# A gated convolution on one core: three weight loads and one output weight, all issued by ScalarE ahead of its table load

## The chip, the cores and the metric

One core of a Trainium2 chip. The metric is device time in microseconds of one execution, median of several runs of the same kernel. A profile is one further execution, recorded by the hardware profiler. It has a span (first to last instruction of the program) that is a little shorter than the device time.

TensorE multiplies, VectorE and ScalarE do elementwise work and move results out of the accumulator banks, GpSimd does a share of the elementwise work, and SyncE only issues transfers. ScalarE can issue transfers too. SyncE's transfers run on the queue that the profile calls q1, ScalarE's on q10.

## The reference

A causal convolution over time with three taps and a dilation of 2, a gate, and an output projection. With B = 2, T = 16000, D = 256, all in bf16:

```python
xp = jnp.pad(x, ((0, 0), (4, 0), (0, 0)))
h  = einsum(xp[:, 4:4+T], w[0]) + einsum(xp[:, 2:2+T], w[1]) + einsum(xp[:, 0:T], w[2])
f, g = h[..., :D], h[..., D:]
z  = tanh(f) * sigmoid(g)
out = z @ w_o
```

`w[k]` is 256 x 512 (256 KB), `w_o` is 256 x 256 (128 KB).

## The kernel before

A row is four time steps, with the phases 0 to 3. Phases 0 and 1 are called x, phases 2 and 3 y; with a dilation of 2, each output of x needs x of its row, y of the row before (`yp`) and x of the row before (`xp`), and each output of y needs y and x of its row and `yp`. Rows are handled in groups of 256 (128 at some ends), and one group of 256 rows is one 512-column product. Channels lie on the partitions, which needs x transposed. That is done by transposing transfers: `load_chunk` (L96 to L108) issues one on SyncE's queue at L105 for each chunk of one or two groups. The first group's 128 rows are handled in another way: they are loaded plainly into `xn` (L117), transposed by TensorE (`turn`, L136 to L143) and copied by ScalarE and VectorE into the first chunk's tile.

The three taps of two outputs are computed with four products and not six. For each group VectorE and GpSimd form the difference m (`pre_m`, L155), the sum p (`pre_p`, L161) and further differences d (`pre_d`, L172). The weights of these products are made once from the taps: `wd0` = 2 w0 and `wd2` = 2 w2 on ScalarE (L363, L364), `wt` = w0 + w2, `wm` = wt - w1 and `wp` = wt + w1 on VectorE (L365 to L367). `products` (L197) multiplies m into a bank b and p into a bank a; `copy_m2` (ScalarE, L227) copies b; `combine` (VectorE, L234 and L235) writes a - copy into b and a + copy into a; then `products` adds d with `wd0` into b and d with `wd2` into a. So TensorE's second pair of products for a block waits for VectorE's combine. A block is 128 of the 512 output channels of a group, four blocks to a group. `activate` (ScalarE, L248) applies tanh or sigmoid, `gate` (VectorE, L266) multiplies, `out_mm` (TensorE, L287) projects with `wo_sb`, and `out_evict` (L306, L308) copies the result out and issues its transfer on SyncE.

The first group (four blocks) doesn't use m, p and d. `direct` (L216) multiplies its rows by the three taps as they come: tap 2 first, then tap 0, then tap 1 (`TAPS = (2, 0, 1)`, L47).

The order of instructions on each engine is the order in which the code is written (`manual_schedule`). The head of the kernel, by engine:

- SyncE issues xn, then tap 0 (L121), then the transposing transfers of chunks 1 and 2 (L105). A third one waits in the loop for its buffer.
- ScalarE issues tap 2 and tap 1 (L119), loads its activation table (L120), copies two of the four turned pieces of x (L143), scales two taps (L363, L364), activates block 0, issues w_o (L375) and activates on.
- VectorE copies the other two pieces of x (L143), makes wt, wm and wp (L365 to L367), then m and p of group 1 (L155, L161), three of its differences, and the first combine.
- TensorE runs 28 products on zeros (L92), turns x (L141), multiplies blocks 0 to 2 by the taps and block 3 by the first two, then takes the m and p products of block 4, the rest of block 3, and in the loop those of blocks 5 and 6 ahead of the d products of block 4.

Each transfer has its own semaphore, and the first instruction on each engine that reads what it loads waits for it.

Of the kernel before, what the change touches and what calls it, by code (L numbers as in the profile page):

```python
# [13 lines left out]
def kernel(  # L14
# [19 lines left out]
    nc = tc.nc  # L34
# [4 lines left out]
    P = 128  # L39
# [7 lines left out]
    TAPS = (2, 0, 1)  # L47
# [41 lines left out]
    def warm_up(n):  # L89
        wps = ps_a.tile([P, 2 * RG], f32, name="a")  # L90
        for _ in range(n):
            nc.tensor.matmul(wps[:, :P], lhsT=warm[:], rhs=warm[:], start=True, stop=True)  # L92
# [20 lines left out]
    w_taps = [consts.tile([P, CT, D2], bf16, name=f"w{k}_sb") for k in range(K)]  # L113
    wo_sb = consts.tile([P, NT, D], bf16)
    xn = consts.tile([P, 4, D], bf16, name="xn")
    w_in = [w[k].rearrange("(ct c) d -> c ct d", c=P) for k in range(K)]
    nc.sync.dma_start(out=xn[:], in_=x[0, 0:4 * P, :].rearrange("(r j) c -> r j c", j=4))  # L117
    for k in (TAPS[0], TAPS[2]):
        nc.scalar.dma_start(out=w_taps[k][:], in_=w_in[k])  # L119
    nc.scalar.preload_act_table(ACT.Sigmoid)  # L120
    nc.sync.dma_start(out=w_taps[TAPS[1]][:], in_=w_in[TAPS[1]])  # L121
    warm_up(N_WARM[0])
    ident = consts.tile([P, P], bf16)
    make_identity(nc, ident[:])
# [56 lines left out]
    def products(k, which):  # L181
        g, oi = divmod(k, 4)
        G = groups[g]
        o = O_ORDER[oi]
        osl = slice(o * P, (o + 1) * P)
        R = G["R"]
        N = 2 * R
        if which in (1, 2):
            G["ab"[which - 1], oi] = (ps_a, ps_b)[which - 1].tile([P, 2 * RG], f32, name="ab"[which - 1])
        wmat, mv, bank, first = {  # L190
            2: (wm_sb, lambda ct: G["m"][:, :, ct, :R], "b", True),
            1: (wp_sb, lambda ct: G["p"][:, :, ct, :R], "a", True),
            3: (wd0_sb, lambda ct: G["d"][:, 2:4, ct, :R], "b", False),
            0: (wd2_sb, lambda ct: G["d"][:, 0:2, ct, :R], "a", False),
        }[which]
        for ct in range(CT):
            nc.tensor.matmul(  # L197
                G[bank, oi][:, :N], lhsT=wmat[:, ct, osl], rhs=mv(ct),
                start=first and ct == 0, stop=ct == CT - 1, skip_group_check=True,
            )  # L200
# [21 lines left out]
    def copy_m2(k):  # L222
        g, oi = divmod(k, 4)
        G = groups[g]
        N = 2 * G["R"]
        G["ss", oi] = ss_pool.tile([P, 2 * RG], f32, name="ss")
        nc.scalar.copy(out=G["ss", oi][:, :N], in_=G["b", oi][:, :N])  # L227
# [9 lines left out]
    def activate(k):  # L237
        g, oi = divmod(k, 4)
        G = groups[g]
        R = G["R"]  # L240
        o = O_ORDER[oi]
        if oi == 0:
            G["th"] = act_pool.tile([P, NT, 4, RG], bf16, name="th")
            G["sg"] = act_pool.tile([P, NT, 4, RG], bf16, name="sg")
            G["z"] = z_pool.tile([P, NT, 4, RG], bf16, name="zz")
        dst = G["th"][:, o] if o < NT else G["sg"][:, o - NT]
        for h, bank in ((1, "b"), (0, "a")):
            nc.scalar.activation(  # L248
                out=dst[:, 2 * h:2 * h + 2, :R],
                in_=G[bank, oi][:, :2 * R].rearrange("p (q r) -> p q r", q=2),  # L250
                func=ACT.Tanh if o < NT else ACT.Sigmoid, scale=1.0 if g == 0 else 0.5,
            )
# [118 lines left out]
    direct(3, TAPS[:-1])  # L371
    products(N_DIRECT, 2)
    products(N_DIRECT, 1)
    activate(0)
    nc.scalar.dma_start(out=wo_sb[:], in_=w_o.rearrange("(ct c) d -> c ct d", c=P))  # L375
    activate(1)
    activate(2)
    copy_m2(N_DIRECT)
    for part in range(3):
        last = pre_d(1, part, nc.vector)  # L380
# [8 lines left out]
    k = N_DIRECT + 1  # L389
# [81 lines left out]
```

## Time and profile before

| | us |
|---|---|
| median of 3 runs | 284.5 (284.37 to 284.89) |
| the profiled execution | 284.21 |
| its span | 282.4 |
| ScalarE busy | 261.0 |
| VectorE busy | 243.2 |
| GpSimd busy | 126.2 |
| TensorE's granted clock | 0.999 of full speed |

A trace lists each instruction with its engine, source line, start and length, the idle time before it and what ended that. For transfers it gives the issue on the issuing engine, the time from the start of the issue to the landing (when the semaphore is complete), and the traffic of each queue in any stretch of time. A matmul's end is modelled, so successive matmuls overlap in the listing; the distance between their starts is what one costs. "Issue" as a releaser means that the engine waited for nothing that the profile shows.

### The profile page before, as it was taken

The page shows a single profiled execution, that of the slowest core. Times are in us where ns is not written, and L with a number is a line of the kernel's source. Part 1 is how long each engine was busy: PE and PEld are TensorE (multiplying, and loading weights), DVE is VectorE, ACT ScalarE, POOL GpSimd, SP SyncE. Part 2 cuts the span into 40 slices and gives each one's busy share as a digit, 9 for nine tenths or more (in the row PEclk, how much of TensorE's full clock was granted, in tenths as well). Part 3 has the DMA queues.
Part 4 walks back from the last instruction along what each step waited for, and adds up shares of the span by engine and source line. Part 5 has one row for each costly group of instructions (what it writes and reads, how often), then busy time and mean ns, then how long its engine had stood idle before and what let it go on. Part 6 is the DMA issues. An engine that isn't in the chain of part 4 may idle for free.

```text
span 282.4 us, 4903 instructions
## 1 busy us (share of the span) xinstructions
PE 277.7 (98%) x1641; PEld 160.3 (57%) x1641; DVE 243.2 (86%) x417; ACT 261.0 (92%) x533; POOL 126.2 (45%) x136
## 2 busy tenths in 40 slices
PE   8999999999999999999999999999999999999994
PEld 8644555555555555556854555555555555555782
DVE  3999888888888888888999988888888888888884
ACT  5598999999999999999999999999999999999994
POOL 1145454455445444533564544554455445443430
PEclk9999999999999999999999999999999999999999
DMA  7887291723718145092793614709345152321223
GB/s 219 191 182 153 75 194 74 172 95 93 184 64 172 67 104 90 37 223 77 183 266 76 171 42 118 182 37 183 121 104 163 50 151 77 79 75 74 77 88 110
DMA packets 76440, 34.55 MB, mean 122 GB/s; under 512 B 66944, under 2 KB 68480, under 8 KB 76416
## 3 DMA queue, kind: packets, MB, share of 16 engines
q1 hardware_dynamic: 75600, 33.59, 48.1%
q10 hardware_dynamic: 816, 0.66, 0.7%
q8 instruction: 13, 0.21, 0.3%
q14 instruction: 11, 0.09, 0.1%
HBM read 1.18 MB, written 16.38 MB: 62 GB/s over the span
## 4 chain that ended last, share of the span: by engine, by line
PE 98%; DVE 0%; DVEq 0%; issue 0%
PE a L197 38%; PE b L197 38%; PE o_ps L287 19%; PE a L92 1%; PE a L216 1%; PE b L216 1%; PE tp L141 0%; PE a L332 0%; DVE osb_end L339 0%; PE b L332 0%; DVEq L466 0%; DVE warm L112 0%
## 5 line engine op out<-in xcount | busy, mean ns | idle before, releaser
L172 POOL TENSOR_TENSOR dd<-xt 128x512 bf16<-128x512 bf16 (+2 forms) x128 | 125.4, 980 | 146.2 <-DVE zz L266 65.5
L234 DVE TENSOR_TENSOR b<-a,ss 128x512 f32<-128x512 f32 (+2 forms) x132 | 87.4, 662 | 30.4 <-ACT ss L227 27.4
L235 DVE TENSOR_TENSOR a<-a,ss 128x512 f32<-128x512 f32 (+2 forms) x132 | 86.2, 653 | 0.0
L227 ACT COPY ss<-b 128x512 f32<-128x512 f32 (+2 forms) x132 | 73.9, 560 | 11.6 <-ACT th L248 0.9
L197 PEld LDWEIGHTS <-wd_sb 128*128 128x128 bf16 x528 | 51.5, 98 | 55.2 <-issue 0.8
L197 PE MATMUL a<-dd,wd_sb 128*128 128x512 bf16 (+2 forms) x264 | 74.7, 364 | 0.0
L197 PE MATMUL b<-dd,wd_sb 128*128 128x512 bf16 (+2 forms) x264 | 74.7, 364 | 0.0
L197 PE MATMUL a<-pp,wp_sb 128*128 128x512 bf16 (+2 forms) x264 | 74.7, 364 | 0.0
L197 PE MATMUL b<-mm,wm_sb 128*128 128x512 bf16 (+2 forms) x264 | 74.7, 364 | 0.0
L287 PE MATMUL o_ps<-wo_sb,zz 128*128 128x256 bf16 x488 | 73.2, 273 | 0.0
L306 ACT CAST osb<-o_ps 128x512 bf16<-128x512 f32 x121 | 72.0, 595 | 0.0
L287 PEld LDWEIGHTS <-zz 128*128 128x128 bf16 x488 | 47.7, 98 | 28.1
L266 DVE TENSOR_TENSOR zz<-th,sg 128x1024 bf16<-128x1024 bf16 (+1 forms) x67 | 43.1, 644 | 0.0
L248 ACT ACTIVATE th<-b 128x512 bf16<-128x512 f32 (+2 forms) x68 | 39.7, 584 | 2.7 <-PE b L197 1.6
L197 PEld LDWEIGHTS <-wp_sb 128*128 128x128 bf16 x264 | 25.8, 98 | 27.3 <-DVE pp L161 0.2
L248 ACT ACTIVATE sg<-b 128x512 bf16<-128x512 f32 (+2 forms) x68 | 39.6, 583 | 0.5 <-PE b L216 0.3
L248 ACT ACTIVATE th<-a 128x512 bf16<-128x512 f32 (+2 forms) x68 | 39.8, 585 | 0.0
L248 ACT ACTIVATE sg<-a 128x512 bf16<-128x512 f32 (+2 forms) x68 | 39.7, 583 | 0.0
L197 PEld LDWEIGHTS <-wm_sb 128*128 128x128 bf16 x264 | 25.8, 98 | 4.5
L161 DVE TENSOR_TENSOR pp<-xt 128x1024 bf16<-128x1024 bf16 (+2 forms) x33 | 21.8, 662 | 0.0
L155 DVE TENSOR_TENSOR mm<-xt 128x1024 bf16<-128x1024 bf16 (+2 forms) x33 | 21.5, 650 | 0.3 <-DMA xt<-in_x_dram 0.3
L216 PEld LDWEIGHTS <-w_sb 128*128 128x128 bf16 x48 | 4.6, 98 | 1.0 <-issue 0.2
(35 smaller groups left out, 36.7 us busy)
## 6 DMA issues: line engine op xcount, KB each, us to landing
out_dram<-osb SPq DMA_DIRECT2D x61, 256.0 KB, 2.1
w_sb<-in_w_dram ACTq DMA_DIRECT2D x2, 256.0 KB, 4.3
xt<-in_x_dram SPq DMA_TRANSPOSE x18, 6.7
xn<-in_x_dram SPq DMA_DIRECT2D x1, 256.0 KB, 3.0
w_sb<-in_w_dram SPq DMA_DIRECT2D x1, 256.0 KB, 4.1
out_dram<-osb_end SPq DMA_DIRECT2D x2, 128.0 KB, 1.9
wo_sb<-in_w_o_dram ACTq DMA_DIRECT2D x1, 128.0 KB, 4.9
out_dram<-osb_odd SPq DMA_DIRECT2D x8, 16.0 KB, 3.0
```

The source lines that it names most:

```text
L155: return nc.vector.tensor_tensor(out=G["m"][:, :, :, :G["R"]], in0=xc, in1=yp, op=ALU.subtract)
L161: return nc.vector.tensor_tensor(out=G["p"][:, :, :, :G["R"]], in0=xc, in1=yp, op=ALU.add)
L172: ins = eng.tensor_tensor(out=G["d"][:, j, :, :R], in0=a[:, q], in1=s[:, q], op=ALU.subtract)
L197: nc.tensor.matmul(G[bank, oi][:, :N], lhsT=wmat[:, ct, osl], rhs=mv(ct), start=first and ct == 0, stop=ct == CT - 1, skip_group_check=True,)
L216: nc.tensor.matmul(G[bank, oi][:, :2 * R], lhsT=w_taps[tap][:, ct, osl], rhs=mv[:, :, ct, :], start=tap == TAPS[0] and ct == 0, stop=tap = ...
L227: nc.scalar.copy(out=G["ss", oi][:, :N], in_=G["b", oi][:, :N])
L234: nc.vector.tensor_tensor(out=pb[:, :N], in0=pa[:, :N], in1=ss[:, :N], op=ALU.subtract)
L235: nc.vector.tensor_tensor(out=pa[:, :N], in0=pa[:, :N], in1=ss[:, :N], op=ALU.add)
L248: nc.scalar.activation(out=dst[:, 2 * h:2 * h + 2, :R], in_=G[bank, oi][:, :2 * R].rearrange("p (q r) -> p q r", q=2), func=ACT.Tanh if o ...
L266: return nc.vector.tensor_tensor(out=G["z"][:, dt, :, :full], in0=G["th"][:, dt, :, :full], in1=G["sg"][:, dt, :, :full], op=ALU.mult)
L287: nc.tensor.matmul(o_ps[:, q, :], lhsT=lhsT, rhs=wo_sb[:, dt, :], start=(dt == 0), stop=(dt == NT - 1),)
L306: copy(out=osb[:, 2 * jp:2 * jp + 2, :], in_=o_ps[:])
```

## The change

Two edits. At the start, the load of tap 0 leaves SyncE's queue and is issued by ScalarE between tap 2 and tap 1 (its three issues then stand in the order 2, 0, 1), and the load of w_o is issued by ScalarE right behind them, ahead of the load of the activation table. SyncE's queue then holds xn and behind it the transposing transfers. Later, the w_o load between the activations of blocks 0 and 1 is gone.

```diff
     nc.sync.dma_start(out=xn[:], in_=x[0, 0:4 * P, :].rearrange("(r j) c -> r j c", j=4))
-    for k in (TAPS[0], TAPS[2]):
+    for k in TAPS:
         nc.scalar.dma_start(out=w_taps[k][:], in_=w_in[k])
+    nc.scalar.dma_start(out=wo_sb[:], in_=w_o.rearrange("(ct c) d -> c ct d", c=P))
     nc.scalar.preload_act_table(ACT.Sigmoid)
-    nc.sync.dma_start(out=w_taps[TAPS[1]][:], in_=w_in[TAPS[1]])
     warm_up(N_WARM[0])
...
-    activate(0)
-    nc.scalar.dma_start(out=wo_sb[:], in_=w_o.rearrange("(ct c) d -> c ct d", c=P))
-    activate(1)
-    activate(2)
+    for k in range(3):
+        activate(k)
     copy_m2(N_DIRECT)
```

The order of all instructions that compute stays the same on every engine.

## The prediction

> **What bounds the kernel now.** I read the page first: busy times and the chain that ended last.
>
> ```profile
> PE 277.7 (98%) x1641; PEld 160.3 (57%) x1641; DVE 243.2 (86%) x417; ACT 261.0 (92%) x533; POOL 126.2 (45%) x136
> PE 98%; DVE 0%; DVEq 0%; issue 0%
> ```
>
> TensorE is busy for 277.7 of 282.4 us, and the chain is TensorE's instruction stream from end to end. The edit touches only transfers that are issued before the loop, so it counts as far as it makes TensorE wait in the first 30 us. The chain in order of time, from 9 to 30 us, shows where it waits today (start, length, what; a pair of 512-column products takes 0.43):
>
> ```profile
> 14.01 0.43 PE b L197 x2
> 14.44 0.57 PE a L197 x2
> ...
> 16.74 0.51 PE a L197 x2
> ...
> 22.49 0.50 PE a L197 x2
> ```
>
> Together with 20.71 (0.48) and 24.28 (0.50), the excess over 0.43 is 0.14 at 14.44 and 0.08 + 0.05 + 0.07 + 0.07 = 0.27 after it. These are products that add into a bank which VectorE's combine (L235) must leave first, and one that waits for a difference (L172). So in the head TensorE is tied to VectorE. The timeline of the other engines says what VectorE and ScalarE are tied to (start, length, engine, line; in brackets the idle time before and what ended it):
>
> ```profile
> 1.75 1.28 ACT L120 ACT_TABLE_LOAD   x1 [1.75 <-issue]
> 4.40 0.80 ACT L143 COPY xt<-tp 128x256 bf16<-128x256 bf16 x2 [1.37 <-PE tp L141]
> 5.36 1.23 DVE L365 TENSOR_TENSOR wt_sb<-w_sb 128x1024 f32<-128x1024 bf16 x1
> 6.62 1.22 DVE L366 TENSOR_TENSOR wm_sb<-wt_sb,w_sb 128x1024 bf16<-128x1024 f32 x1
> ...
> 10.24 0.24 PEld L197 LDWEIGHTS <-wp_sb 128*128 128x128 bf16 x2 [0.19 <-DVE pp L161]
> ...
> 14.70 0.70 DVE L155 TENSOR_TENSOR mm<-xt 128x1024 bf16<-128x1024 bf16 x1 [0.34 <-DMA xt<-in_x_dram]
> ```
>
> From L365 at 5.36 VectorE has no idle time until 14.36, and TensorE's weight load for the first p product already waits for it at 10.24. So a late start of L365 (needs taps 0 and 2) or of L366 (needs tap 1) passes on. At 14.70 VectorE waits 0.34 for the second transposed chunk, and then has no idle time until 28.3.
>
> Last, the queues. SyncE's issues, ScalarE's w_o, and then issue to landing of single transfers (stretches 0.5 to 1, 1.5 to 1.7, and 6 to 12 us):
>
> ```profile
> 1.19 0.42 SPq L121 DMA_DIRECT2D w_sb<-in_w_dram  x1
> 1.66 4.31 SPq L105 DMA_TRANSPOSE xt<-in_x_dram  x1
> 6.02 4.54 SPq L105 DMA_TRANSPOSE xt<-in_x_dram  x1
> 8.37 0.37 ACTq L375 DMA_DIRECT2D wo_sb<-in_w_o_dram  x1
> ```
>
> ```profile
> w_sb<-in_w_dram ACTq DMA_DIRECT2D x1, 256.0 KB, 3.7
> xn<-in_x_dram SPq DMA_DIRECT2D x1, 256.0 KB, 3.0
> ...
> w_sb<-in_w_dram SPq DMA_DIRECT2D x1, 256.0 KB, 4.1
> w_sb<-in_w_dram ACTq DMA_DIRECT2D x1, 256.0 KB, 4.8
> xt<-in_x_dram SPq DMA_TRANSPOSE x1, 7.1
> ...
> wo_sb<-in_w_o_dram ACTq DMA_DIRECT2D x1, 128.0 KB, 4.9
> ```
>
> Issue plus landing: xn 0.73 + 3.0 = 3.73; tap 2 0.73 + 3.7 = 4.43; tap 0 1.19 + 4.1 = 5.29; tap 1 about 1.24 + 4.8 = 6.04; first chunk (T1) 1.66 + 7.1 = 8.76; second chunk (T2) 6.02 + 8.7 = 14.7; w_o 8.37 + 4.9 = 13.3. The four plain loads land in the order in which they were issued, whichever queue they are on. Tap 0 lands within 0.1 us of its first users, and tap 1 0.6 us ahead of L366.
>
> **The row that decides.** The w_o load was issued on ScalarE's queue while T2 was in progress on SyncE's. Traffic by queue, q1 being SyncE's and q10 ScalarE's, in 9.8 to 11.8 us and then in 11.8 to 12.6 us (packets, MB, share of 16 engines):
>
> ```profile
> q1 hardware_dynamic: 2265, 0.58, 127.4%
> ```
>
> ```profile
> q10 hardware_dynamic: 272, 0.13, 59.8%
> q1 hardware_dynamic: 145, 0.03, 18.3%
> ```
>
> The xn load moves its first bytes within 1.3 to 1.8 us of issue (the stretch 2.0 to 2.5 is the first with traffic). The w_o load moves nothing until 11.8, which is 3.4 us, and then all of itself as T2 runs out. A plain load that comes behind a transposed one waits the transposed one out, on the other queue too.
>
> **The change, part by part.**
>
> Tap 0 moves from SyncE's second place to ScalarE's second. Its issue starts at about 1.22 (0.73 plus one issue of 0.49) and not at 1.19: nothing by itself. But SyncE's T1, which stood behind it (issue at 1.66), now starts at about 1.19, 0.47 earlier and beside or ahead of tap 0. I take it that T1 gets ahead, because it starts 0.03 earlier; nothing in the trace shows the tie itself. By the w_o row tap 0 then waits T1 out. T1's last bytes came at about 7.5 (traffic falls there to half, between T1 and T2), behind taps 0 and 1. These take 0.26 MB at 378 GB/s each (the rate in 3.3 to 4.9 us), 0.69 us. Without them T1 ends at 7.5 - 1.4 = 6.1, or 5.9 by its last full-rate stretch (7.3); I take 5.95. Then tap 0: 0.69 of traffic and 0.35 to the landing (tap 1's last traffic was before 5.7, and it landed at 6.04) make 7.0, against 5.29. L365 starts at 7.0 and not at 5.36: **+1.64 us** on VectorE. TensorE's own need (tap 0 at 6.42) waits 0.6 of that, and the rest at the first m and p products; behind L365 VectorE queues L366, L367, the first m and p, three differences and the combine that TensorE waits for at 14.44, so the whole 1.64 arrives there. Ends of this cost: 0, if tap 0 is ahead of T1 or alternates with it, and 2.1, if tap 0's traffic starts only at T1's landing (the 304-row chunk issued at 225.28 lands after 4.5; 1.19 + 4.5, and 0.69 for tap 2 ahead of T1, is 6.4; tap 0 at 7.45). The row nearest is w_o's, so I take 1.64.
>
> Tap 1's issue moves from 1.24 to 1.72 behind tap 0. With tap 0 at 7.0 it lands at 7.7, before L366 would want it (7.0 + 1.26 = 8.3): hidden under L365. If tap 0 came early it would not be hidden (a rival below).
>
> The transposes move up by 0.47, and T2 with them. T2 needs 1.08 MB at 290 GB/s (the 9.8 to 11.8 stretch), 3.7 us; started behind T1 and taps 0 and 1 (7.35) it ends at 11.1, and lands at 12.3 with T1's tail of 1.2, at 13.6 with its own of today (last bytes at 12.2, landing at 14.7). VectorE's wait of 0.34 at 14.70 goes, in each case below but that of a blocked T2. TensorE's four later excesses hang on the same VectorE stretch: **-0.27 us**. The bound on any gain is all five, 0.41. T1's earlier landing is worth nothing, since VectorE gets to it only at 8.89, straight from L367.
>
> ScalarE: four issues in front of the table load put that from 1.75 to about 0.73 + 4 x 0.49 = 2.7, done at 4.0. The copy at 4.40 covers it with 0.4 to spare. If the fourth issue were held up until T1's issue ends, the copy would come late and TensorE's first products with it; but they wait for tap 0 at 7.0 in that case anyway, so 0.3 at most. L363 and L364 (tap copies) start at 7.0 and end at 9.1; the first activation stood at 8.36 and ScalarE idles 0.46 at 10.58: covered. The w_o issue leaves a place where it cost ScalarE nothing (the activations around 8.37 run back to back), and w_o is first needed at 14.64, so it may stay behind T2 again.
>
> Sum on the profiled run (284.21 us, its span 282.4 and 1.8 around it): 284.21 + 1.64 - 0.27 = 285.6. The three timed runs have a median of 284.5, 0.29 above that run, so **285.9 us**.
>
> The Trainium skill's page "DMA: Bandwidth & Descriptors", section "Queues, rings and completion order", says that each DMA engine serves the queues in turn and changes after one packet, some 9 to 17 descriptors. By it tap 0 would alternate with T1 and land at about 5.3, as now, and the time would be that of the first rival; q10's empty 9.8 to 11.8 us speaks against it here, the alternation of the first four loads for it.
>
> **The rivals.**
>
> Fair alternation, no loss: taps 0 and 1 share the engines with T1 in small turns and land near 5.3 and 6.3, before 5.36 and 6.62. For it: the plain loads of the two queues alternate before 5 us at 378 GB/s. Against: the w_o row. Only the -0.27 is left: 283.9 on the profiled run, 284.2 on the median. This is the case on the other side: the earlier T2 alone decides, from a landing before 14.36 on.
>
> Tap 0 wins the tie, tap 1 is behind T1: T1 then ends at 5.95 + 0.69 = 6.65, tap 1 lands at 6.65 + 0.69 + 0.35 = 7.7 to 7.8, and L366 starts there and not at 6.62: +1.2 - 0.27, 285.1 or 285.4. For it: a lead of 0.03 us is small.
>
> Behind both transposes: T2's issue follows T1's by 0.05 us, and if SyncE's stream is never let go, tap 0 or tap 1 waits 3.7 us more. Tap 1 then lands at about 11.6, L366 is 5.0 late; or L365 5.4 late: 284.21 + 4.7 to 5.1, some 289.4 on the median. Against: w_o got in while 145 packets of T2 were still to come, so a gap between two transposes should do.
>
> **How the numbers follow.** Forecast 0.50; tap 1 alone late 0.14; fair alternation 0.22; behind both 0.12; other 0.02. The range reaches down past the alternation's 284.2 to 284.0, and up to 287.6, which is the forecast's upper end (284.5 + 2.1 + 0.3 = 286.9, with no gain at T2) and 0.7 for a T2 that gets a first part in ahead of tap 1; behind both is left out. The forecast's own range is 285.2 (a T1 shorter by 0.7) to 286.9. A difference of 0.2% (0.57 us) is about what a measurement tells from none: 283.9 to 285.1 is the same. The bound on gains (0.41) leaves 0.06 for faster; alternation gives 0.22 for same; the rest, 0.72, is slower.
>
> **What would show it.** Right: no q10 traffic from about 3.9 us until T1's bytes end near 6; L365 starts near 7.0 with idle time before it put down to the tap load; L363 likewise; the chain shows TensorE waiting near 6.4 and again for the first m and p; VectorE's wait at T2 gone; from 30 us on both traces alike but for the shift. Wrong: q10 busy together with q1's small packets before 6 us, and L365 at 5.4. The size is wrong if T1 takes longer or shorter than 2.3 us once it starts, or if T2 slips in before tap 1.

## The result and the profile after

The changed kernel takes 286.99 us (median of 6 runs, 285.80 to 287.57) against 284.44 (6 runs, 284.15 to 284.89): a ratio of 1.0083, 95% interval 1.0058 to 1.0108. It is 2.55 us slower. Its profiled execution took 287.56 us with a span of 285.8, 3.4 more than the span of before; it is one of the two longest of the six, so its loss is larger than that of the medians.

The page of the changed kernel, busy times and chain that ended last:

```profile
PE 278.5 (97%) x1641; PEld 160.1 (56%) x1641; DVE 242.9 (85%) x417; ACT 261.1 (91%) x533; POOL 126.2 (44%) x136
PE 94%; DMA 3%; DVE 1%; ACTq 0%; DVEq 0%; issue 0%
```

The chain is no longer TensorE's from end to end: 3% of it is a transfer. In order of time (start, length, what):

```profile
1.23 0.49 ACTq L119
1.72 0.03 issue
1.75 8.36 DMA w_sb<-in_w_dram
...
10.20 1.23 DVE wm_sb L366
11.43 1.14 DVE wp_sb L367
12.57 0.61 DVE mm L155
13.18 0.05 issue
13.23 0.61 PE b L197 x2
...
17.91 0.59 PE a L197 x2
```

The transfer is ScalarE's third issue, tap 1. It lands 8.36 us after its issue at 1.75, at 10.11, where it landed at 6.04 before. The timeline of the engines shows who waits:

```profile
5.25 1.21 DVE L365 TENSOR_TENSOR wt_sb<-w_sb 128x1024 f32<-128x1024 bf16 x1
10.15 2.12 PEld L216 LDWEIGHTS <-w_sb 128*128 128x128 bf16 x20 [2.09 <-DMA w_sb<-in_w_dram]
10.20 1.23 DVE L366 TENSOR_TENSOR wm_sb<-wt_sb,w_sb 128x1024 bf16<-128x1024 f32 x1 [3.73 <-DMA w_sb<-in_w_dram]
```

L365, which needs tap 0, starts at 5.25 (5.36 before). L366, which needs tap 1, starts at 10.20 (6.62 before), 3.58 later. The product that waits for the first combine starts at 17.91 (14.44 before), 3.47 later. Behind it the pairs longer than 0.43 sum to 0.14 (25.86 and 27.65), and not 0.27. 3.47 - 0.13 is 3.34, the 3.4 of the two spans.

The first transposing load (T1) and the last two weights of the same execution, then the traffic by queue in 6 to 9 us (packets, MB, share of 16 engines), then stretches of 1 us (engines' busy time, clock, share of the transfer engines, GB/s):

```profile
1.19 3.80 SPq L105 DMA_TRANSPOSE xt<-in_x_dram  x1
```

```profile
w_sb<-in_w_dram ACTq DMA_DIRECT2D x1, 256.0 KB, 8.4
wo_sb<-in_w_o_dram ACTq DMA_DIRECT2D x1, 128.0 KB, 8.3
xt<-in_x_dram SPq DMA_TRANSPOSE x1, 9.6
```

```profile
q10 hardware_dynamic: 254, 0.21, 65.5%
q1 hardware_dynamic: 608, 0.15, 54.5%
```

```profile
4.00:5.00 1.00, 1.00 (x11) 0.85 (x8) 0.29 (x1) 0.61 (x3) 0.00 (x0) 1.00 1.21 296
6.00:7.00 1.00, 1.00 (x11) 0.82 (x10) 0.47 (x1) 1.00 (x2) 0.00 (x0) 1.00 1.21 127
7.00:8.00 1.00, 1.00 (x12) 0.90 (x10) 0.00 (x0) 0.14 (x1) 0.00 (x0) 1.00 1.21 134
```

This is the new thing in the trace. From 6 to 9 us both queues move, and the transfer engines count as busy as ever (share 1.21), but they carry 0.36 MB in 3 us, about 120 GB/s. The plain loads alone made 378 GB/s, a transposing load alone, once in flow, 290. T1 suffers too: it lands 9.6 us after its issue, at 10.8 (8.76 before), though it was issued 0.47 earlier. I call this the crawl below.

It does not begin with T1's first bytes. Traffic of the changed kernel in 4.6 to 5.3 us, where ScalarE's queue (q10) moves nothing, and then a stretch of the kernel before, in which T2 starts and q10 moves nothing either:

```profile
q1 hardware_dynamic: 711, 0.18, 128.2%
```

```profile
8.00:8.50 0.50, 0.50 (x7) 0.44 (x6) 0.50 (x1) 0.14 (x1) 0.00 (x0) 1.00 1.11 118
```

So T1 first flows alone at 260 GB/s while tap 1 waits, and the crawl sets in when tap 1's first bytes come, at 5.3. And a low rate at a high share is not by itself a sign of two queues: at the start of T2 one queue alone made 118 GB/s at a share of 1.11. There it is soon over (115 GB/s in 7.4 to 8.5 us, 289 from 8.75 on); in the change it lasts for three microseconds and more.

### The profile page after: what moved, and what is told of

The parts are those of the page before. It is cut to its first block, busy times and chain, and to the rows that moved or that the text cites. A ratio compares the mean times of both kernels' runs of the same rounds, so it can differ in the third digit from the quotient of the medians.

```text
span 285.8 us, 4902 instructions
## 1 busy us (share of the span) xinstructions
PE 278.5 (97%) x1641; PEld 160.1 (56%) x1641; DVE 242.9 (85%) x417; ACT 261.1 (91%) x533; POOL 126.2 (44%) x136
## 3 DMA queue, kind: packets, MB, share of 16 engines
HBM read 1.18 MB, written 16.38 MB: 61 GB/s over the span
## 4 chain that ended last, share of the span: by engine, by line
PE 94%; DMA 3%; DVE 1%; ACTq 0%; DVEq 0%; issue 0%
PE a L197 37%; PE b L197 37%; PE o_ps L287 19%; DMA w_sb<-in_w_dram 3%; DVE wm_sb L366 0%; DVE wp_sb L367 0%; ACTq L119 0%; DVE mm L155 0%; PE a L332 0%; DVE osb_end L339 0%; PE b L332 0%; DVEq L464 0%; PE a L216 0%; PE b L216 0%; DVEq L366 0%
```

## The experiments

Three theories were set against each other. **Order:** T1's issue now stands ahead of tap 1's, so the two are on the way together. **Volume:** w_o, as one more plain load beside T1, draws it out. **Queue:** ScalarE's queue is slow for its later loads. Line numbers in these runs are shifted by up to two against the kernel before. Times are medians, with the ratio to the kernel before on the same chip; in the last columns are the issue of T1, and issue and landing of tap 1 in the profiled execution.

| run | median us | ratio (95%) | T1 issued | tap 1 issued | tap 1 landed |
|---|---|---|---|---|---|
| change | 286.99 | 1.0083 (1.0058 to 1.0108) | 1.19 | 1.75 | 10.1 |
| w_o late | 287.05 | 1.0082 (1.0055 to 1.0109) | 1.20 | 1.75 | 10.9 |
| w_o alone early | 284.69 | 1.0006 (0.9994 to 1.0018) | 1.66 | 1.2 | 6.0 |
| tap 1 on SyncE | 284.88 | 1.0018 (1.0009 to 1.0027) | 1.66 | 1.20 | 5.3 |
| T1 held | 285.02 | 1.0015 (1.0005 to 1.0026) | 3.17 | 1.75 | 6.0 |
| short hold | 289.29 | 1.0173 (1.0155 to 1.0191) | 1.62 | 1.74 | 11.1 |
| half a us behind | 284.79 | 1.0018 (1.0006 to 1.0030) | 2.29 | 1.75 | 6.0 |
| "after the table load" | 286.85 | 1.0078 (1.0063 to 1.0093) | 1.19 | 1.78 | 8.9 |
| tap 1 behind T1, SyncE | 285.86 | 1.0051 (1.0037 to 1.0065) | 1.20 | 5.03 | 8.2 |
| tap 1 late, ScalarE | 285.71 | 1.0041 (1.0023 to 1.0058) | 1.18 | 4.84 | 8.3 |

**w_o back in its late place.** Half of the change undone.

```diff
     for k in TAPS:
         nc.scalar.dma_start(out=w_taps[k][:], in_=w_in[k])
-    nc.scalar.dma_start(out=wo_sb[:], ...)
...
     activate(0)
+    nc.scalar.dma_start(out=wo_sb[:], ...)
     activate(1)
```

> The changed kernel with w_o's load back between the activations of blocks 0 and 1; the three taps stay on ScalarE. Theory 1 (order: T1's issue starts at 1.19, ahead of tap 1's at 1.75, so the two move side by side and tap 1 comes late): tap 1 still lands near 9.5 to 10.1, 286.5 to 287. Theory 2 (volume: w_o as a second plain load beside T1 is what draws the crawl out): tap 1 lands by 8 us, L366 waits at most 1.5, 285.4.

The loss is all there without w_o beside T1, and tap 1 lands at 10.9. Volume is out.

**w_o alone moved early.** The other half.

```diff
     for k in (TAPS[0], TAPS[2]):
         nc.scalar.dma_start(out=w_taps[k][:], in_=w_in[k])
+    nc.scalar.dma_start(out=wo_sb[:], ...)
     nc.scalar.preload_act_table(ACT.Sigmoid)
     nc.sync.dma_start(out=w_taps[TAPS[1]][:], in_=w_in[TAPS[1]])
```

> The kernel before with w_o's load alone moved in front of the table load (ScalarE's third issue, at about 1.72, beside T1's at 1.66); tap 0 stays on SyncE. Theory 1: all three taps are issued ahead of T1 and land as before (4.4, 5.3, 6.0), w_o may be late without harm, but T1 is slowed beside it: T1 lands up to 1 us later, 284.5 to 285.5. Theory 2: w_o beside T1 is the trouble, T1 lands at 10 or later, and the first m waits over 1 us: 285.5 or more.

No difference is measured. w_o was issued at 1.74, 0.08 behind T1, and yet landed in 4.8 us with T1 in 7.2, as without it. So an issue just behind T1's is not enough for a crawl. Here T1 stood behind tap 0 on its own queue. Its first bytes come at 5.1, w_o's at 5.0, and most of w_o moves in 5.0 to 5.5 us:

```profile
q10 hardware_dynamic: 233, 0.12, 78.9%
q1 hardware_dynamic: 91, 0.02, 20.3%
```

**Tap 1 on SyncE, tap 0 on ScalarE.**

```diff
-    for k in (TAPS[0], TAPS[2]):
+    for k in TAPS[:2]:
         nc.scalar.dma_start(out=w_taps[k][:], in_=w_in[k])
     nc.scalar.preload_act_table(ACT.Sigmoid)
-    nc.sync.dma_start(out=w_taps[TAPS[1]][:], in_=w_in[TAPS[1]])
+    nc.sync.dma_start(out=w_taps[TAPS[2]][:], in_=w_in[TAPS[2]])
```

> Taps 2 and 0 on ScalarE, tap 1 on SyncE ahead of the transposing loads (T1's issue back at 1.66), w_o late as before. Theory 1: every tap is issued ahead of T1, so tap 0 lands near 4.9, tap 1 near 5.3 to 6, 284.2 to 284.5, as before. A theory that ScalarE's queue is itself slow for the second load: tap 0 late, L365 after 5.4, over 284.8.

My numbers for the two landings were the wrong way round: SyncE's load, issued 0.03 ahead, went first (tap 1 at 5.3) and ScalarE's second came behind it (tap 0 at 6.1), so L365 started at 6.20. But there is no crawl, and 0.84 us of lateness at L365 cost 0.2% of the time.

**T1 held behind all four weights.** Nothing else of the change is touched; GpSimd writes half of the tile that T1 fills, and T1 waits for that.

```diff
         if c == 0:
             return
+        if c == 1:
+            nc.gpsimd.memset(xt[:, 0:2, :, :], 0.0)
```

> The changed kernel with one GpSimd memset over half of the second chunk's tile, which T1 must wait for: T1's issue moves from 1.19 to about 2.8, behind the issue of all four weights. Theory 1: tap 1 lands near 5.9 to 6.2 and L366 starts at 6.5, T1 lands near 9.2, so the first m waits some 0.3 to 0.5: 284.5 to 285. Theory 2 or one by which four loads on ScalarE's queue are slow themselves: tap 1 lands after 7, 285.5 or more.

Issue to landing of tap 1 and of T1 in this run:

```profile
w_sb<-in_w_dram ACTq DMA_DIRECT2D x1, 256.0 KB, 4.3
...
xt<-in_x_dram SPq DMA_TRANSPOSE x1, 6.5
```

With four weights on ScalarE's queue and T1 at 3.17, tap 1 lands 4.3 us after its issue. The queue theory is out. What is left of the loss, 0.15%, has its own place in the trace: T1 lands 6.5 after 3.17, and the first m waits 0.84 for it at 9.74.

**A short hold, then half a microsecond.** The same memset over 256 columns of the tile, and, with w_o late, over 1056.

```diff
+        if c == 1:
+            nc.gpsimd.memset(xt[:, 0, 0, 0:256], 0.0)
```

```diff
+        if c == 1:
+            nc.gpsimd.memset(xt[:, 0, :, :], 0.0)
```

> The changed kernel with a short GpSimd memset (256 columns) into the second chunk's tile: T1's issue moves from 1.19 to about 1.6 to 1.75, where it stood in the kernel before, still 0 to 0.15 us ahead of tap 1's issue at 1.75. If the early start of T1 is the whole cause (T1 0.55 ahead of tap 1), tap 1 lands near 6 and L366 starts near 6.5: 284.3 to 284.9. If T1 being issued ahead of tap 1 at all is enough: tap 1 lands after 8, 286 or more.

> The three taps on ScalarE, w_o late, and T1 held by a GpSimd memset of 1056 columns until about 2.2 to 2.4, half a microsecond behind tap 1's issue at 1.75 (0.12 ahead of it in the run with the short hold, 0.55 ahead in the change). If the order of these two issues decides: tap 1 lands near 6, T1 near 8.9 to 9.2, VectorE waits at most 0.3: 284.2 to 284.7, the whole loss gone. If a crawl needs only that plain loads still have bytes to move when T1 begins: tap 1 lands after 8, 286 or more.

T1 at 1.62, about where it stood in the kernel before, does not help: 0.12 ahead of tap 1 gives the worst time of all. Not all of that is the crawl itself. Tap 1 lands 1.0 later than in the change (11.1), but the profiled execution is 1.8 longer. TensorE had waited 3.18 us for tap 1; from 12 to 14 us it was granted half the clock, and its pairs of 256-column products take 0.43 and not 0.22. The stretch from 12 to 13 us (granted clock 0.50, third from the end) and one such pair:

```profile
12.00:13.00 1.00, 1.00 (x7) 0.69 (x5) 1.00 (x2) 1.00 (x4) 0.00 (x0) 0.50 1.28 291
```

```profile
12.36 0.43 PE a L218 x2
```

In the profiled execution of the change, where TensorE waited 1.81, the pairs behind the wait start 0.22 apart. T1 at 2.29, 0.54 behind tap 1, has tap 1 down in 4.3 us and T1 in 6.4, at 8.7, about as in the kernel before. Between 0.12 ahead and 0.54 behind, the crawl goes; the turning point inside was not looked for. The two runs differ in w_o as well, but w_o was early in the run with T1 at 3.17 too, which has no crawl. The 0.18% that is left is not T1's or tap 1's: VectorE has no idle time from L365 until the first combine (see the last section).

**Tap 1 "after the table load".**

```diff
-    for k in TAPS:
+    for k in TAPS[:2]:
         nc.scalar.dma_start(out=w_taps[k][:], in_=w_in[k])
-    nc.scalar.dma_start(out=wo_sb[:], ...)
     nc.scalar.preload_act_table(ACT.Sigmoid)
+    nc.scalar.dma_start(out=w_taps[TAPS[2]][:], in_=w_in[TAPS[2]])
+    nc.scalar.dma_start(out=wo_sb[:], ...)
```

> The changed kernel with tap 1 and w_o issued behind the table load, tap 1 at about 3.05, 1.9 us after T1's issue and not 0.55. If a plain load that comes well into a transposing one waits for its end without slowing it (as w_o did behind T2 in the kernel before), T1 runs at full rate to about 6.6 and tap 1 lands at 7.6 to 8: L366 at 8, 285.3 to 285.8, faster than the change. If any plain load beside T1 makes both crawl, tap 1 lands at 10 or later: 287 or more.

This did not test what it was made for. ScalarE's timeline in this run:

```profile
1.75 1.28 ACT L120 ACT_TABLE_LOAD   x1 [1.75 <-issue]
1.78 0.46 ACTq L121 DMA_DIRECT2D w_sb<-in_w_dram  x1
2.27 0.49 ACTq L122 DMA_DIRECT2D wo_sb<-in_w_o_dram  x1
```

The issue does not wait for the table load in front of it, so the loads go out as in the change, and the time is the change's. As another profile of the change's order, it shows how the crawl varies: tap 1 took 7.1 us here, 8.4 in the change and 9.1 and 9.4 in the two other runs with it. The ten timed runs with w_o late lie between 285.09 and 288.74; those of the kernel before within 1.4 us of each other.

**Tap 1 behind T1 on the same queue.**

```diff
     for c in range(2):
         load_chunk(c)
+    nc.sync.dma_start(out=w_taps[TAPS[2]][:], in_=w_in[TAPS[2]])
     load_chunk(2)
```

> Taps 2 and 0 on ScalarE, w_o late, T1 issued at 1.19, and tap 1 issued by SyncE behind T1 on the same queue. If the crawl comes from two queues being served in small turns: no crawl here, T1 runs at 290 GB/s once begun and lands by 8, tap 1 behind it at 7.6 to 8.2: L366 at about 8, 285.2 to 285.8, faster than the change though tap 1 stands later in line. If tap 1's lateness were just its place behind T1's bytes, it is as late as in the change: 10, 287.

Traffic of this run in 4.5 to 6 us, and issue to landing of T1 and of tap 1:

```profile
q1 hardware_dynamic: 1689, 0.43, 127.3%
q10 hardware_dynamic: 2, 0.00, 0.2%
```

```profile
xt<-in_x_dram SPq DMA_TRANSPOSE x1, 5.8
...
w_sb<-in_w_dram SPq DMA_DIRECT2D x1, 256.0 KB, 3.2
```

With the other queue empty T1 runs at 0.43 MB in 1.5 us, 290 GB/s, and lands at 7.0. Tap 1 is issued at 5.03 and lands at 8.23, sooner than the change's, which was issued 3.3 us earlier.

**Tap 1 late on ScalarE's queue.** Issued behind ScalarE's copies of x.

```diff
     for j in range(4):
         turn(j)
+    nc.scalar.dma_start(out=w_taps[TAPS[2]][:], in_=w_in[TAPS[2]])
     warm_up(N_WARM[1])
```

> Taps 2 and 0 on ScalarE, w_o late, T1 issued at 1.19, and tap 1 issued by ScalarE only behind its two copies of x, at about 5.2 and not at 1.75, with T1 in full flow. If a plain load that comes into a flowing transposing one waits for its end and doesn't slow it (as w_o did behind T2), T1 ends near 6.3 at 290 GB/s and tap 1 lands at 7.6 to 8.2, some 2 us sooner than in the change though it is issued 3.4 us later: L366 near 8, 285.2 to 286. If two queues beside each other always crawl: tap 1 lands after 9, 286.5 or more.

Traffic of this run in 4.5 to 5.9 us, and the chain of waits:

```profile
q1 hardware_dynamic: 1468, 0.38, 125.6%
q10 hardware_dynamic: 19, 0.01, 2.4%
```

```profile
4.84 3.41 DMA w_sb<-in_w_dram
```

So the other queue alone is not it either. Tap 1, issued when T1 is in full flow, lands 3.41 us after its issue, and T1 is not slowed (6.0 to its landing). Whether it had to wait for T1's end, as w_o did behind T2, this run hardly tells: its first bytes come at 6.5, 1.7 us after its issue, which is no later than xn's (1.3 to 1.8), and T1's last come at 6.6. The run with tap 1 behind T1 on SyncE's queue changed two things, the queue and the time of the issue; as the time alone does as much, that run does not show that the crawl needs two queues.

The traces of these runs, laid side by side, differ in which load moves first. In the four with the crawl (the change, w_o late, the short hold, "after the table load") T1's first bytes come at 4.2 to 4.5 and tap 1's at 4.7 to 5.3. In the kernel before and in the runs with w_o alone early, tap 1 on SyncE, T1 held and T1 half a microsecond behind, the last load on ScalarE's queue that was issued near T1 (tap 1, w_o or tap 0) starts 0.1 to 1.0 ahead of T1's first bytes. This tells the runs apart where the order of the issues doesn't (w_o 0.08 behind T1: no crawl; tap 1 0.12 behind T1: the longest). It is read from the traces; no run changed it alone.

**Extra plain loads in the loop.** One 256 KB load on ScalarE's queue, into a tile that nothing reads, near each transposing load of the kernel before.

```diff
+        if load and loaded % 3 == 0:
+            nc.scalar.dma_start(out=extra[:], in_=w_in[0])
         if k < NB:
             activate(k - 1)
+        if (load and loaded % 3 == 1) or late:
+            nc.scalar.dma_start(out=extra[:], in_=w_in[0])
+        late = load and loaded % 3 == 2
```

> The kernel before with one extra 256 KB plain load (tap 2's weights form, into a tile that nothing reads) issued by ScalarE near each transposing load of the loop, in turn a little ahead of, with and some 2 us behind its issue; nothing but transfers and ScalarE's issue time is added. If a plain load issued shortly after a transposing one makes both crawl, those transposing loads take 9 to 10 us to land (alone 6.4 to 6.8) and the plain ones over 6; those issued well into it wait for its end (3 to 5 us) with the transposing one at its usual 6.7. If the crawl belongs to the kernel's first microseconds alone, all land in 6.4 to 7.5. The time rises by up to 0.5 us in either case.

One execution took 285.49 us. Issue to landing of the pairs in it, by who was issued first. In brackets stand the plain load's issue time and, in the last column, what the same transposing load took in the kernel before, without the plain one:

| plain load issued | plain, us | transposing, us |
|---|---|---|
| 1.48 ahead (49.77) | 2.7 | 6.6 (6.6) |
| 0.27 ahead (68.28) | 3.4 | 6.9 (6.6) |
| 0.27 ahead (120.20) | 3.3 | 6.7 (6.4) |
| 0.26 ahead (208.85) | 3.3 | 6.8 (6.7) |
| 0.80 behind (136.69) | 5.2 | 7.8 (7.1) |
| 1.89 behind (87.75) | 4.9 | 7.5 (7.2) |
| 1.95 behind (35.89) | 7.3 | 9.4 (7.9) |
| 1.90 behind (228.32) | 3.7 | 5.8 (4.5) |
| 1.90 behind (176.40) | 5.0 | 7.0 (6.8) |
| 3.21 behind (156.98) | 4.0 | 7.3 (6.8) |

Four more stood 1.4 to 1.5 ahead (2.6 to 2.9, and one 4.4), two behind the transposing load's issue by 3.6 and 5.1 (3.5 and 2.8). A plain load that is issued a quarter of a microsecond ahead costs the transposing one about 0.3 at most. Within 3.2 us behind, it takes 3.7 to 7.3 us and the transposing load 0.2 to 1.5 more. The order holds outside the kernel's first microseconds too, but a crawl as long as the change's came only once here (35.89), and not for the nearest offset behind, 0.80. My expectation of 9 to 10 us for those was wrong.

**w_o behind T2, and both orders together.** The kernel before with w_o as SyncE's issue behind T2; and the run with T1 half a microsecond behind tap 1 with the same.

```diff
     load_chunk(2)
+    nc.sync.dma_start(out=wo_sb[:], ...)
     loaded = 3
```

> The kernel before with w_o's load issued by SyncE behind the second transposing load (issue at about 10.6) and not by ScalarE at 8.37. T2 then ends undisturbed at about 12.1, lands before 14.36, and VectorE's wait of 0.34 goes; w_o lands near 13.5, ahead of its use at 14.6. If TensorE's later excess of 0.27 hangs on that wait: 284.2, 0.1% faster than before. If not: 284.5.

> The run with T1 half a microsecond behind tap 1, and w_o issued by SyncE behind T2. If both orders help as far as they can: L365 at 5.25 and not 5.36, VectorE's wait for T2 gone: 284.1, 0.1 to 0.15% under the kernel before, which this many rounds may or may not tell. If T1 comes too late by the hold, 284.5 to 284.9.

284.31 us, ratio 0.9993 (0.9983 to 1.0004), and 284.69, ratio 1.0010 (0.9998 to 1.0021): neither is told from the kernel before, and no run here beats it. In the second, tap 1 took 5.0 us and T1 7.0, where the run with the same order above had 4.3 and 6.4. VectorE's wait for T2 is gone in both. But three of the four later excesses stay: with w_o behind T2 the chain has 0.46, 0.50 and 0.50 at 21.00, 22.75 and 24.55, so only the first, 0.08, had hung on that wait.

## Why the prediction was right, and where it was not

The forecast was slower, 285.9 in a range of 284.0 to 287.6; measured was 286.99. The direction and the path of the loss were reasoned and held. That the time lies in the range is in part luck: the range's top was made for a long T1 and for a T2 that slips in, the forecast's own range ended at 286.9, and the load that was late is another than the one in the sum. By the prediction's own signs the forecast's mechanism failed: L365 started at 5.25 and not near 7.0, and q10 moves beside T1's small packets from 5.3 on. Point by point:

- **That T1's early issue costs weights their place, and that this passes through VectorE to TensorE: right.** Holding T1 alone brings tap 1 back from 10.1 to 6.0. The lateness at L366, 3.58 us, is still 3.47 at the product behind the first combine, as the sum had it.
- **That T1 gets ahead of tap 0: wrong.** Tap 0 landed at 5.1 and L365 started at 5.25; tap 1 was the one caught. That was the second rival's place, to which I gave 0.14. A lead of 0.03 us at the issue was no ground to choose by: T1 moves its first bytes only at about 4.2, with most of tap 0 through.
- **That the one caught waits T1 out: so for about a microsecond, then wrong, and it set the size.** The w_o row showed a plain load that came 2.35 us into T2. Tap 1 comes 0.55 behind T1's issue; it waits until 5.3, when T1 is about half through, and from there both crawl. The rival's price, +1.2, took tap 1 at 7.8 with T1 at full rate; measured was 10.1 and +3.6. With tap 1 issued at 4.84 and 5.03, T1 does run at full rate and tap 1 lands at 8.3 and 8.2.
- **That tap 1 then has time behind tap 0: not tested,** since tap 0 was on time.
- **-0.27 for the earlier T2: too much.** VectorE's wait for T2 did go. The excess fell by 0.13 here, and with w_o behind T2 by little more than the one pair of 0.08.
- **ScalarE's four issues: right.** The table load moved to 2.79, done at 4.07; the copy still starts at 4.41, with 0.33 idle ahead of it in place of 1.37. w_o landed at 10.6, and its lateness cost nothing.
- **Fair alternation: half seen.** The Trainium skill's page "DMA: Bandwidth & Descriptors", section "Queues, rings and completion order", has the engines serve the queues in turn. The trace agrees in so far as q1 and q10 both move from 6 to 9 us; from 4.6 to 5.3 it does not, since q10, with tap 1 issued at 1.75, moves nothing. That taking turns is free, as this rival had it, the trace denies: 120 GB/s.

What happens inside the transfer engines in the crawl is not shown. It is shown that it goes when T1 alone is issued later, that it goes when tap 1 is issued well into T1, and that w_o is not needed for it. That it takes two queues fits all runs, but no run shows it by itself.

## What to carry to other kernels

Spreading loads so that a transposing transfer starts earlier can cost the plain loads that are issued beside it several microseconds. In these runs it was safe to issue what is needed first a quarter to half a microsecond or more ahead of the transposing transfer, and far better to issue it well behind (tap 1 landed at 8.2 and 8.3, on either queue) than 0.1 to 0.6 us behind on the other queue (tap 1 landed at 8.9 to 11.1). In a trace, look for two queues that both move while the GB/s fall to a third at an unchanged engine share for longer than the 1.1 us that it took at the start of T2 by itself, and look which of the two moved first. A second queue is no gain where the first one's order was what kept a long transfer behind the short ones.

## What the runs showed that I had not expected

Issuing a transposing load occupies SyncE for microseconds, and for longer in the first ones: T1's issue takes 4.31 us behind tap 0 in the kernel before and 3.80 in the change, against 2.30 for a longer one at 225.28. That the loads ahead of it hold it up is likely, but no run shows it.

TensorE's first 256-column products run at either of two rates, and when it changes varies by execution. The six tap 2 products at 5.1 us take 0.80 in the profile of before and 1.38 in the run with T1 half a microsecond behind tap 1, and the next six 0.67 and 0.97, at a granted clock of 1.00 in both by the profile. These are pieces of the chain of waits of the latter:

```profile
5.11 1.38 PE a L217 x6
6.49 0.97 PE b L217 x6
7.47 0.22 PE a L217 x2
```

In that run TensorE reaches the first m product at 11.00 and not at 10.12, with nothing waiting for a load. The Trainium skill's page "TensorE: Matmul & The Clock Gate", section "Part 1: The HAM clock gate", says that TensorE starts at half rate and leaves it at the end of a free-running window of some 3.4 us, so that the moment varies by run. These rows agree in the two rates (0.23 us a product at first in the latter, 0.11 later) and in that the moment varies; none of them shows the window. It is a part of the spread between runs of one kernel. Whether it is all of the 0.18% left in that run stays open.
